# Block-sparse attention and a mixer MLP on one core: steps of two key chunks, and QK in 64-row tiles with the mask as a product

## The chip, the cores and the metric

The kernel runs on one core of a Trainium2 chip. The time is device microseconds of one execution on that core, from three timed runs; beside them stands one profiled execution, from which all durations of instructions come. TensorE (PE in the profile; PEld is its weight load) multiplies matrices into PSUM, ScalarE (ACT) and VectorE (DVE) work elementwise and are the two that empty PSUM, GpSimd (POOL) issues the casting loads, and SyncE (SP) issues the other transfers, among them the transposes by the DMA crossbar.

## The reference

Inputs q, k, v have shape (4, 8, 768, 64): 4 batches, 8 heads, 768 positions, 64 dimensions. Positions form 24 blocks of 32.

```python
scores = scale * np.matmul(q, k.transpose(0, 1, 3, 2))        # scale = 1/8
mask = np.abs(blk_i - blk_j) <= 1
mask = mask | (blk_i == 0) | (blk_j == 0) | (blk_i == 23) | (blk_j == 23)
for qb in range(24):
    for kb in sampled_blocks[qb]:                             # 3 random blocks
        mask[qb*32:(qb+1)*32, kb*32:(kb+1)*32] = True
attn = softmax(np.where(mask, scores, -1e9))
x = (attn @ v), heads side by side                            # (4, 768, 512)
h = np.maximum(x.transpose(0, 2, 1) @ w_tok1, 0) @ w_tok2     # token MLP, 768 -> 256 -> 768
u = x + h.transpose(0, 2, 1)
out = u + np.maximum(u @ w_ch1, 0) @ w_ch2                    # channel MLP, 512 -> 1536 -> 512
```

## The kernel before

**Attention** goes by pairs of heads, 16 pairs (`p`), four to a batch. q and k of a pair are loaded as bf16, brought into layout on VectorE (L533, `klay`, `qlay`), turned by TensorE (L593) and copied out of PSUM by VectorE, each head by itself, into rows 0 to 63 of `ktb` and `qtb` (L608). Rows 64 to 87 of both hold the mask as 24 more rows of the contraction: `ktb` has the indicator of the key's block, `qtb` has -30000 where the query may not see the block and 0 where it may. So one matmul over 88 rows gives masked scores. From pair 10 (`NPE`) on the turning is done by the DMA crossbar instead (L559), out of `wide` tiles in which the mask rows were laid once (`wide_stream`, L487 to L499).

A step is `(p, half, j)`: one key chunk of 128 (`j`, six of them) against 384 queries, for both heads. QK (L639) puts the transposed scores, keys in rows, into `ps`, two matmuls of 384 columns; ScalarE takes the exponential into `et` (L648, 768 elements a row, no maximum subtracted). PV (L692) then takes `et` as weights, 128 queries at a time, against v with a column of ones (65 columns), and accumulates in `po` over the six key chunks: six matmuls a step. After the sixth, VectorE takes the reciprocal of the sums (L706) and multiplies it in (L707), which gives `x`.

**The MLP** of a batch: the token MLP by halves of the channels (`tok`, L770, L795, addition L803), turning of `u` (for the first batch by TensorE, L824, later by crossbar, L750), then the channel MLP (`ch`): 96 matmuls of 384 columns (L862) with ReLU on ScalarE (L734) or VectorE (L736), and 72 of 512 columns (L888) with the residual addition on VectorE (L897) and the output transfer.

**The order of the instructions** is found when the program is built. A planner (`Planner`) plays the engines with assumed costs in ns and emits an instruction when its inputs and its buffer would be ready. TensorE takes the ready stream of lowest number: QK 0, PV 1, transposes 2, token MLP 3, channel MLP 4. The other engines take the ready operation with the lowest `prio`; ScalarE takes nothing but exponentials while one is pending (`exp_pending`). On the chip the order of each engine stays as it was planned, and semaphores hold an instruction whose inputs are late.

**Buffers:** `ps` two tiles of two PSUM banks, `po` one, `pm` three banks for everything else on TensorE; `et` eight tiles (`NET`); `ktb`, `qtb`, `vaug` four pairs each (`NV`).

Of the kernel before, what the change touches and what calls it, by code (L numbers as in the profile page):

```python
# [169 lines left out]
def kernel(  # L170
# [22 lines left out]
    NET = 8  # L193
    NPE = 10
    NL = 2
# [16 lines left out]
    wide = {  # L212
        (nm, n): sb1.tile([128, 2, NC, 128], BF16, name=f"{nm}wide{n}")
        for n in range(NL) for nm in ("k", "q")
    }

# [211 lines left out]
    wide_there = {(nm, n): Ev() for nm in ("k", "q") for n in range(NL)}  # L428
# [49 lines left out]
    def wide_stream():  # L478

        box, done, rel = {}, Ev(), Ev()  # L480

        def emit():
            P.take("pm", rel)
            box["m"] = psM.tile([128, 2, NC, 24], FP32, tag="pm", name="pm_wide")
            for i, rhs in enumerate((ident[R, 64:88], t2add[R, :])):
                for c in range(NC):
                    nc.tensor.matmul(  # L487
                        out=box["m"][:, i, c, :], lhsT=ind[R, c, :], rhs=rhs,
                        start=(i == 0 and c == 0), stop=(i == 1 and c == NC - 1),
                    )  # L490

        yield 500.0, [Ev(62 * US)], [("pm", 1)], emit, done
        for n in range(NL):
            for i, nm in enumerate(("k", "q")):
                def clear(eng, nm=nm, n=n):
                    nc.vector.memset(wide[nm, n][:, :, :, 64:128], 0.0)

                def copy(eng, nm=nm, n=n, i=i):
                    nc.vector.tensor_copy(  # L499
                        out=wide[nm, n][:, :, :, 64:88],  # L500
                        in_=free(box["m"][:, i, 0, :], 0, [[0, 2], [24, NC], [1, 24]]),
                    )
                ev = P.op(("dve",), {"dve": 420.0}, [Ev(60 * US)], clear, prio=6)
                ev = P.op(("dve",), {"dve": 450.0}, [done, ev], copy, prio=6)
                wide_there[nm, n].same_as = ev
                rel.same_as = ev

# [12 lines left out]
    def relayout(p):  # L520
        lays = {}
        for nm in ("k", "q", "v") if p else ("v",):
            raw = raws.pop((nm, p))
            arr = arrive.pop((nm, p))

            def emit(eng, nm=nm, raw=raw):
                if nm == "v":
                    nc.vector.tensor_copy(out=vaug[p % NV][:, :, :, 0:64], in_=raw[:, :, :, :])  # L528
                elif p >= NPE:
                    nc.vector.tensor_copy(out=wide[nm, p % NL][:, :, :, 0:64], in_=raw[:, :, :, :])  # L530
                else:
                    lay = sbw.tile([128, NC, 2, D], BF16, tag=f"{nm}lay", bufs=1, name=f"{nm}lay{p}")
# [10 lines left out]
            if nm != "v" and p >= NPE:  # L543
                deps.append(wide_there[nm, p % NL])
                if p - NL >= NPE:
                    deps.append(xb_done[nm, p - NL])
# [5 lines left out]
    xb_done = {}  # L552

    def crossbar(p):

        lays = relayout(p)
        for nm, bufs, there in (("k", ktb, kT_there), ("q", qtb, qT_there)):
            def emit(eng, nm=nm, bufs=bufs):
                nc.sync.dma_start_transpose(  # L559
                    out=bufs[p % NV][:, :, :].rearrange("e h (c s) -> e (h c) s", c=NC),  # L560
                    in_=wide[nm, p % NL][:, :, :, :].rearrange("p h c e -> p (h c e)"),
                )
            deps = [lays[nm + "ev"]]
            if p >= NV:
                deps.append(qk_done[p - NV])
            ev = P.op(("sp",), {"sp": 1600.0}, deps, emit, prio=1, lat=5000.0)
            xb_done[nm, p] = ev
            there[p, 0], there[p, 1] = ev, ev

    def transposes(p):  # L570
# [15 lines left out]
        for nm, bufs, there in (("k", ktb, kT_there), ("q", qtb, qT_there)):  # L586
            box, last, rel = {}, Ev(), Ev()
            for c in range(NC):
# [10 lines left out]
                if p >= NV:  # L599
                    deps.append(qk_done[p - NV])  # L600
                yield 56.0, deps, [("pm", 1)] if c == 0 else [], emit, last if c == NC - 1 else None
            for hd in range(2):
# [15 lines left out]
    steps = [(p, half, j) for p in range(NP) for half in range(2) for j in range(NC)]  # L618
# [4 lines left out]
    for s in steps:  # L623
        et_there[s] = Ev()

    def qk_stream():
        for s in steps:
            p, half, j = s
            yield lambda p=p: (p, 1) in qT_there
            done, rel = Ev(), Ev()  # L630

            def emit(s=s, done=done, rel=rel):
                p, half, j = s
                P.take("ps", rel)
                P.take("et", et_rel[s])
                ps = psS.tile([128, 2, 512], FP32, tag="ps", name=f"ps{p}_{half}_{j}")
                for hd in range(2):
                    n = p % NV
                    nc.tensor.matmul(  # L639
                        out=ps[:, hd, 0:384], lhsT=ktb[n][0:88, hd, 128 * j : 128 * j + 128],  # L640
                        rhs=qtb[n][0:88, hd, 384 * half : 384 * half + 384],
                        start=True, stop=True,
                    )
                P.exp_pending += 1

                def exp(eng):
                    et = sbw.tile([128, 2, 384], BF16, tag="et", bufs=NET, name=f"et{p}_{half}_{j}")
                    nc.scalar.activation(  # L648
                        out=et[:, :, :], in_=ps[:, :, 0:384], func=AF.Exp, scale=0.125
                    )  # L650
                    ets[s] = et
                    P.exp_pending -= 1

                ev = P.op(("act",), {"act": 735.0}, [done], exp, prio=0, lat=80.0)
                alias(et_there[s], ev)
                alias(rel, ev)

            if p == 0:
                deps = [f_there["k", j // 3], f_there["q", half]] + [rows_there[0]] * half
            else:  # L660
                deps = [e for hd in range(2) for e in (kT_there[p, hd], qT_there[p, hd])]
                if p < NPE:
                    deps.append(rows_there[p % NV])
            yield (
                326.0, deps,
                [("ps", 1), ("et", 1)], emit, done,
            )
            if half == 1 and j == NC - 1:
                alias(qk_done[p], done)

    et_rel = {s: Ev() for s in steps}

    def pv_stream():
        for s in steps:
            p, half, j = s
            done = et_rel[s]

            def emit(s=s, done=done):
                p, half, j = s
                b, pb = p // 4, p % 4  # L680
                et = ets.pop(s)
                if j == 0:
                    rel = Ev()
                    P.take("po", rel)
                    po_of[p, half] = (
                        psO.tile([128, 2, 3, 65], FP32, tag="po", name=f"po{p}_{half}"), rel
                    )
                po, rel = po_of[p, half]
                va = vaug[p % NV]
                for hd in range(2):  # L690
                    for c in range(3):
                        nc.tensor.matmul(  # L692
                            out=po[:, hd, c, :],
                            lhsT=et[:, hd, 128 * c : 128 * c + 128],
                            rhs=va[:, hd, j, 0:65],
                            start=(j == 0 and hd == 0 and c == 0),
                            stop=(j == NC - 1 and hd == 1 and c == 2),
                        )
                if j < NC - 1:
                    return  # L700

                def norm(eng):
                    if b not in xs:
                        xs[b] = sbw.tile([128, 2, NC, 256], BF16, tag="x", bufs=B, name=f"x{b}")
                    recip = sbw.tile([128, 2, 3], FP32, tag="recip", name=f"recip{p}_{half}")
# [3 lines left out]
                            xs[b][:, pb // 2, 3 * half, 128 * (pb % 2) : 128 * (pb % 2) + 128], 0,  # L709
                            [[64, 2], [256, 3], [1, 64]],  # L710
                        ),
                        in0=po[:, :, :, 0:64],
                        in1=free(recip[:, :, :], 0, [[3, 2], [1, 3], [0, 64]]),
# [3 lines left out]
                ev = P.op(("dve",), {"dve": 760.0}, [done], norm, prio=1)  # L717
                alias(rel, ev)
                alias(x_there.setdefault((p, half), Ev()), ev)

            yield lambda p=p: p in va_there
            yield 176.0, [et_there[s], va_there[p], ones_there[p % NV]], [("po", 1)] if j == 0 else [], emit, done
            if half == 1 and j == NC - 1:
# [36 lines left out]
    def tok(b, g):  # L760
        deps = [x_there[2 * g + 4 * b + i, h] for i in range(2) for h in range(2)] + [tok1_there]
# [155 lines left out]
    for p in range(NP):  # L917
        for h in range(2):
            x_there[p, h] = Ev()
# [19 lines left out]
    P.stream(-1, wide_stream())  # L939
# [57 lines left out]
```

## Time and profile before

| | before |
|---|---|
| timed runs | 273.66, 272.22, 271.15 us; median 272.22 |
| profiled execution | 271.31 us, of which the span from first to last instruction is 269.6 |
| granted TensorE clock | 0.999 |
| busy: PE, ACT, DVE, POOL | 262.9, 184.8, 118.8, 42.2 us |
| QK (L639) | 384 matmuls of 384 columns |
| exponentials (L648) | 192 of 768 elements, 810 ns |
| PV (L692) | 1152 matmuls of 65 columns |
| channel MLP (L862, L888) | 384 of 384 columns; 276 of 512, 12 of 256, 24 of 128 |

A page of the profile gives busy time by engine, the busy share of 40 slices of the span as a digit in tenths, and the chain that ended last: the work followed back from the last instruction, at each step to what released it. A group row reads: line, engine, operation, tile written <- tiles read, shape, count | busy us of the group, mean ns of one | idle us of the engine before them, and what ended that idle time. In the chain in order of time a row is: start us, us, what. A row of windows gives for each engine its busy us and, in brackets, its instructions, in the order PE, PEld, DVE, ACT, POOL, then the granted clock, the DMA share and GB/s. Matmuls are pipelined and the end of one is modelled, so their busy times overlap, and the distance from start to start is what one costs.

### The profile page before, as it was taken

What the parts mean: (1) busy time and instruction counts of PE and PEld (TensorE: products, weight loads), DVE (VectorE), ACT (ScalarE), POOL (GpSimd) and SP (SyncE); (2) the same over time, 40 slices, a digit from 0 to 9 for tenths busy, and PEclk for the clock granted to TensorE, in tenths of its full rate; (3) what the DMA queues carried; (4) which work ended last, traced back from release to release, by engine and by line L of the source; (5) the groups of instructions that cost most, each with busy time, mean ns of one, the idle gap of its engine ahead of it and who ended that gap; (6) DMA issues with size and microseconds to landing.
All of it is one profiled execution on the core that took longest, in us unless ns stands there. A gap on an engine that the chain in (4) does not pass through costs nothing.

```text
span 269.6 us, 6198 instructions
## 1 busy us (share of the span) xinstructions
PE 262.9 (98%) x2595; PEld 170.5 (63%) x2595; DVE 118.8 (44%) x269; ACT 184.8 (69%) x274; POOL 42.2 (16%) x66
## 2 busy tenths in 40 slices
PE   8898999999999999999999999999999999999995
PEld 3476777776777767777677664565445654465444
DVE  7878878696954563634435433200231002200122
ACT  5899999999999999999999910177004750077200
POOL 8746555561221000000000000000000000000000
PEclk9999999999999999999999999999999999999999
DMA  6999999999799863971300036300122002310123
GB/s 153 187 217 202 213 201 206 202 201 137 98 202 154 164 100 74 177 80 39 62 2 2 0 61 175 116 1 2 46 109 80 0 0 86 111 41 0 41 82 113
DMA packets 48476, 27.90 MB, mean 103 GB/s; under 512 B 29696, under 2 KB 44816, under 8 KB 48448
## 3 DMA queue, kind: packets, MB, share of 16 engines
q0 software_dynamic: 15104, 12.98, 31.0%
q1 hardware_dynamic: 33072, 14.33, 22.7%
q8 instruction: 20, 0.33, 0.5%
q10 hardware_dynamic: 272, 0.20, 0.3%
q14 instruction: 8, 0.07, 0.1%
HBM read 26.74 MB, written 6.29 MB: 123 GB/s over the span
## 4 chain that ended last, share of the span: by engine, by line
PE 80%; ACT 14%; DVE 3%; issue 1%; DMA 1%; ACTq 0%; DVEq 0%
PE pm_ch L862 23%; PE pm_ch L888 22%; PE ps L639 17%; ACT et L648 14%; PE po L692 9%; PE pm_tok L795 3%; PE pm_tok L770 3%; PE ps_idle L299 2%; DMA out_dram<-o 1%; PE tk L593 1%; PE tq L593 1%; DVE ktb L608 0%; DVE qtb L402 0%; PE pm_ut L824 0%; PE pm_e L395 0%
## 5 line engine op out<-in xcount | busy, mean ns | idle before, releaser
L648 ACT ACTIVATE et<-ps 128x768 bf16<-128x768 f32 x192 | 143.7, 810 | 3.1 <-PE ps L639 1.7
L639 PE MATMUL ps<-qtb,ktb 88*128 88x384 bf16 x384 | 93.7, 325 | 1.7 <-ACT et L648 1.1
L734 ACT ACTIVATE rc<-pm_ch 128x384 bf16<-128x384 f32 x74 | 36.3, 491 | 59.3 <-PE pm_ch L862 43.3
L862 PE MATMUL pm_ch<-uT,w_ch 128*128 128x384 bf16 x384 | 72.2, 326 | 0.0
L692 PEld LDWEIGHTS <-et 128*128 128x128 bf16 x1152 | 55.3, 97 | 21.6 <-DVE x L707 1.5
L888 PE MATMUL pm_ch<-w_ch,rc 128*128 128x512 bf16 (+2 forms) x312 | 63.4, 363 | 0.0
L692 PE MATMUL po<-vaug,et 128*128 128x65 bf16 x1152 | 60.4, 193 | 0.4 <-DVE x L707 0.4
L897 DVE TENSOR_TENSOR o<-pm_ch,x 128x512 f32<-128x512 f32 x23 | 15.9, 692 | 88.4 <-PE pm_ch L888 88.4
L888 PEld LDWEIGHTS <-rc 128*128 128x128 bf16 x312 | 29.6, 98 | 31.8
L862 PEld LDWEIGHTS <-w_ch 128*128 128x128 bf16 x384 | 36.2, 98 | 20.9
L639 PEld LDWEIGHTS <-ktb 88*128 88x128 bf16 x384 | 35.0, 98 | 11.6 <-issue 3.0
L803 DVE TENSOR_TENSOR x<-pm_tok,x 128x512 bf16<-128x512 f32 x24 | 15.9, 686 | 11.3 <-PE pm_tok L795 11.2
L707 DVE TENSOR_TENSOR x<-po,recip 128x384 bf16<-128x384 f32 x32 | 17.8, 557 | 1.1
L736 DVE TENSOR_SCALAR rc<-pm_ch 128x384 bf16<-128x384 f32 x22 | 12.2, 553 | 12.5 <-PE pm_ch L862 12.4
L795 PE MATMUL pm_tok<-a_t,w_tok 128*128 128x256 bf16 x96 | 17.1, 276 | 0.0
L706 DVE RECIPROCAL recip<-po 128x6 f32<-128x6 f32 x32 | 6.3, 196 | 23.7 <-PE po L692 23.0
L770 PE MATMUL pm_tok<-x,w_tok 128*128 128x256 bf16 x96 | 16.5, 272 | 0.0
L235 POOL DMA_DIRECT2D vraw<-in_v_dram x16 | 11.6, 725 | 18.6 <-DVE vaug L528 14.5
L235 POOL DMA_DIRECT2D qraw<-in_q_dram x15 | 11.0, 730 | 9.7 <-DVE qwide L530 1.6
L235 POOL DMA_DIRECT2D kraw<-in_k_dram x15 | 10.8, 717 | 8.7 <-DVE recip L706 2.4
L608 DVE COPY ktb<-tk 64x768 bf16<-64x768 bf16 x18 | 9.9, 552 | 3.0 <-PE tk L593 2.8
L795 PEld LDWEIGHTS <-w_tok 128*128 128x128 bf16 x96 | 9.8, 129 | 1.2
(73 smaller groups left out, 103.5 us busy)
## 6 DMA issues: line engine op xcount, KB each, us to landing
out_dram<-o SPq DMA_DIRECT2D x23, 256.0 KB, 2.0
vraw<-in_v_dram POOLq DMA_DIRECT2D x16, 192.0 KB, 7.7
w_ch<-in_moe_w_ch_dram POOLq DMA_DIRECT2D x8, 384.0 KB, 9.8
kraw<-in_k_dram POOLq DMA_DIRECT2D x15, 192.0 KB, 8.6
qraw<-in_q_dram POOLq DMA_DIRECT2D x15, 192.0 KB, 8.0
w_tok<-in_moe_w_tok_dram POOLq DMA_DIRECT2D x2, 384.0 KB, 9.9
kf<-in_k_dram SPq DMA_DIRECT2D x2, 192.0 KB, 3.0
ktb<-ktb SPq DMA_DIRECT2D x3, 72.0 KB
```

Of the source, the lines that this page charges most:

```text
L235: nc.gpsimd.dma_start(out=raw[:, :, :, :], in_=APx(src, 2 * p * S * D, [[NC * D, 128], [S * D, 2], [1, NC * D]]),)
L639: nc.tensor.matmul(out=ps[:, hd, 0:384], lhsT=ktb[n][0:88, hd, 128 * j : 128 * j + 128], rhs=qtb[n][0:88, hd, 384 * half : 384 * half + 38 ...
L648: nc.scalar.activation(out=et[:, :, :], in_=ps[:, :, 0:384], func=AF.Exp, scale=0.125)
L692: nc.tensor.matmul(out=po[:, hd, c, :], lhsT=et[:, hd, 128 * c : 128 * c + 128], rhs=va[:, hd, j, 0:65], start=(j == 0 and hd == 0 and c = ...
L707: nc.vector.tensor_tensor(out=free(xs[b][:, pb // 2, 3 * half, 128 * (pb % 2) : 128 * (pb % 2) + 128], 0, [[64, 2], [256, 3], [1, 64]],), ...
L734: nc.scalar.activation(out=o(), in_=i, func=AF.Relu)
L770: nc.tensor.matmul(out=box["pm"][:, t, :], lhsT=w_tok1[:, sc, 128 * t : 128 * t + 128], rhs=xs[b][:, g, sc, :], start=(t == 0 and sc == 0) ...
L795: nc.tensor.matmul(out=ubox["pm"][:, i, :], lhsT=w_tok2[:, t, :, 2 * s2 + i], rhs=a_t[:, t, :], start=(i == 0 and t == 0), stop=(i == 1 an ...
L803: nc.vector.tensor_tensor(out=st[b]["u"][:, g, 2 * s2 : 2 * s2 + 2, :], in0=ubox["pm"][:, :, :], in1=xs[b][:, g, 2 * s2 : 2 * s2 + 2, :], ...
L862: nc.tensor.matmul(out=pbox["pm"][:, 0:384], lhsT=w_ch1[:, dmc, 128 * cc : 128 * cc + 128], rhs=st[b]["uT"][:, dmc // 2, 3 * sh : 3 * sh + ...
L888: nc.tensor.matmul(out=pbox["pm"][:, 0:n], lhsT=box["rc"][:, cc, 128 * sc : 128 * sc + 128], rhs=w_ch2[:, cc, lo : lo + n], start=(cc == 0 ...
L897: nc.vector.tensor_tensor(out=o[:, :].rearrange("p (g e) -> p g e", g=2), in0=pbox["pm"][:, :].rearrange("p (g e) -> p g e", g=2), in1=st[ ...
```

## The change

A step becomes `(p, t, jj)`: two key chunks (256 keys) against 256 queries, three by three steps a pair. An exponential covers 1024 elements, a PV step has eight matmuls, and `po` is finished three times a pair. In pairs 0 to 5 QK is as before in kind: matmuls over 88 rows, four of 256 columns.

From pair 6 (`NT0`) on the mask rows are gone. `ktb` and `qtb` hold one head in rows 0 to 63 and the other in rows 64 to 127, so a transposed pair is copied out of PSUM at once, and the crossbar of pairs 10 to 15 turns the plain layout. A QK matmul covers 64 rows; the two heads' matmuls lie in different row halves of the array and write different PSUM banks. Two steps are issued together, when both `ps` tiles are free. After the exponential VectorE multiplies `et` in place by a mask of 0 and 1 (the cut, rank 5, the lowest). The mask (128 keys x 6 chunks x 768 queries) is built once, from 34 us of the planner's time on, by 12 matmuls over the 24 mask rows and 12 comparisons on VectorE; everything that overwrites the mask rows waits for it. The wide tiles go. `et` has seven tiles (of 1024 elements) for eight (of 768), and the layout tiles two buffers each for one.

```diff
-    NET = 8
+    NET = 7
     NPE = 10
-    NL = 2
+    NT0 = 6
...
+    def mask_stream():
+        for j in range(NC):
+            for hf in range(2):
...
+                    nc.tensor.matmul(
+                        out=box["m"][:, 0:384], lhsT=ind[R, j, :],
+                        rhs=qtb[0][R, 0, 384 * hf : 384 * hf + 384], start=True, stop=True,
                     )
+                yield 162.5, [Ev(34 * US), rows_there[0]], [("pm", 1)], emit, last
...
+                    nc.vector.tensor_scalar(
+                        out=mask[:, j, 384 * hf : 384 * hf + 384], in0=box["m"][:, 0:384],
+                        scalar1=-1.0, scalar2=None, op0=ALU.is_ge,
+                    )
+                ev = P.op(("dve",), {"dve": 556.0}, [last], copy, prio=4)
...
-            if nm != "v" and 2 <= p < NPE:
-                deps.append(qT_there[p - 1, 1])
+            if nm != "v" and p >= 3:
+                deps.append(qT_there[p - 2, 1])
...
                 nc.sync.dma_start_transpose(
-                    out=bufs[p % NV][:, :, :].rearrange("e h (c s) -> e (h c) s", c=NC),
-                    in_=wide[nm, p % NL][:, :, :, :].rearrange("p h c e -> p (h c e)"),
+                    out=bufs[p % NV][:, 0, :].rearrange("e (c s) -> e c s", c=NC),
+                    in_=lays[nm][:, :, :, :].rearrange("p c h d -> p (c h d)"),
                 )
-            ev = P.op(("sp",), {"sp": 1600.0}, deps, emit, prio=1, lat=5000.0)
+            deps = [lays[nm + "ev"], mask_there, qk_done[p - NV]]
+            ev = P.op(("sp",), {"sp": 900.0}, deps, emit, prio=1, lat=5000.0)
...
+            if p >= NT0:
+                def evac(eng, buf=bufs[p % NV], box=box):
+                    copy = nc.scalar.copy if eng == "act" else nc.vector.tensor_copy
+                    copy(out=buf[:, 0, :], in_=box["t"][:, :, :].rearrange("p c s -> p (c s)"))
...
-    steps = [(p, half, j) for p in range(NP) for half in range(2) for j in range(NC)]
+    steps = [(p, t, jj) for p in range(NP) for t in range(3) for jj in range(3)]
...
+    def scores(s, done, rel):
...
+        for i in range(2):
+            for hd in range(2):
+                rows, h = (slice(0, 88), hd) if p < NT0 else (slice(64 * hd, 64 * hd + 64), 0)
+                nc.tensor.matmul(
+                    out=ps[:, hd, 256 * i : 256 * i + 256],
+                    lhsT=ktb[n][rows, h, 256 * jj + 128 * i : 256 * jj + 128 * i + 128],
+                    rhs=qtb[n][rows, h, 256 * t : 256 * t + 256],
+                    start=(i == 0), stop=(i == 1),
+                )
...
+            nc.scalar.activation(out=et[:, :, :], in_=ps[:, :, :], func=AF.Exp, scale=0.125)
...
+        ev = P.op(("act",), {"act": 948.0}, [done], exp, prio=0, lat=80.0)
+        if p >= NT0:
+            def cut(eng):
+                nc.vector.tensor_tensor(
+                    out=ets[s][:, :, :].rearrange("k h (i q) -> k h i q", i=2),
+                    in0=ets[s][:, :, :].rearrange("k h (i q) -> k h i q", i=2),
+                    in1=free(mask[:, 2 * jj, 256 * t : 256 * t + 256], 0, [[0, 2], [S, 2], [1, 256]]),
+                    op=ALU.mult,
+                )
+            ev = P.op(("dve",), {"dve": 740.0}, [ev, mask_there], cut, prio=5)
...
+                yield (
+                    436.0, qk_deps(*s), [("ps", 1), ("et", 1)],
...
+            def emit(s=s, s2=s2, evs=evs):
+                scores(s, evs[0][0], evs[1][0])
+                scores(s2, evs[0][1], evs[1][1])
...
+            yield 650.0, qk_deps(*s) + qk_deps(*s2), [("ps", 2), ("et", 2)], emit, None
...
-    P.stream(-1, wide_stream())
+    P.stream(1.8, mask_stream())
```

More of the change, by code (lines that the diff above doesn't have):

```diff
@@ L476, in first_rest, with emit, copy @@
             )
[L478 to L486, printed above, removed]
+    mask = sb1.tile([128, NC, S], BF16, name="mask")
+    mask_there = Ev()
+    def mask_stream():
+        for j in range(NC):
+            for hf in range(2):
+                box, last, rel = {}, Ev(), Ev()
+                def emit(j=j, hf=hf, box=box, rel=rel):
+                    P.take("pm", rel)
+                    box["m"] = psM.tile([128, 512], FP32, tag="pm", name=f"pm_mask_{j}_{hf}")
                     nc.tensor.matmul(
-                        out=box["m"][:, i, c, :], lhsT=ind[R, c, :], rhs=rhs,
-                        start=(i == 0 and c == 0), stop=(i == 1 and c == NC - 1),
-                    )
[L492 to L501, printed above, removed]
-                    )
-                ev = P.op(("dve",), {"dve": 420.0}, [Ev(60 * US)], clear, prio=6)
-                ev = P.op(("dve",), {"dve": 450.0}, [done, ev], copy, prio=6)
-                wide_there[nm, n].same_as = ev
+                        out=box["m"][:, 0:384], lhsT=ind[R, j, :],
+                        rhs=qtb[0][R, 0, 384 * hf : 384 * hf + 384], start=True, stop=True,
+                    )
+                yield 162.5, [Ev(34 * US), rows_there[0]], [("pm", 1)], emit, last
+                def copy(eng, j=j, hf=hf, box=box):
+                    nc.vector.tensor_scalar(
+                        out=mask[:, j, 384 * hf : 384 * hf + 384], in0=box["m"][:, 0:384],
+                        scalar1=-1.0, scalar2=None, op0=ALU.is_ge,
+                    )
+                ev = P.op(("dve",), {"dve": 556.0}, [last], copy, prio=4)
                 rel.same_as = ev
+        mask_there.same_as = ev
     def act_cost(n):
@@ L624, with exp @@
         et_there[s] = Ev()
+    et_rel = {s: Ev() for s in steps}
+    def scores(s, done, rel):
+        p, t, jj = s
+        P.take("ps", rel)
+        P.take("et", et_rel[s])
+        ps = psS.tile([128, 2, 512], FP32, tag="ps", name=f"ps{p}_{t}_{jj}")
+        n = p % NV
+        for i in range(2):
+            for hd in range(2):
+                rows, h = (slice(0, 88), hd) if p < NT0 else (slice(64 * hd, 64 * hd + 64), 0)
[5 more added lines that the diff above has]
+                )
+        P.exp_pending += 1
+        def exp(eng):
+            et = sbw.tile([128, 2, 512], BF16, tag="et", bufs=NET, name=f"et{p}_{t}_{jj}")
+            nc.scalar.activation(out=et[:, :, :], in_=ps[:, :, :], func=AF.Exp, scale=0.125)
+            ets[s] = et
+            P.exp_pending -= 1
+        ev = P.op(("act",), {"act": 948.0}, [done], exp, prio=0, lat=80.0)
+        alias(rel, ev)
+        if p >= NT0:
+            def cut(eng):
[6 more added lines that the diff above has]
+            ev = P.op(("dve",), {"dve": 740.0}, [ev, mask_there], cut, prio=5)
+        alias(et_there[s], ev)
@@ L626, in qk_stream, with qk_deps @@
+    def qk_deps(p, t, jj):
+        if p > 0:
+            deps = [e for hd in range(2) for e in (kT_there[p, hd], qT_there[p, hd])]
+            return deps + [rows_there[p % NV]] * (p < NT0)
+        deps = [f_there["k", int(jj > 0)], f_there["q", int(t > 0)]]
+        return deps + [rows_there[0]] * (t > 0)
     def qk_stream():
-        for s in steps:
-            p, half, j = s
+        todo = list(steps)
+        while todo:
+            s = todo.pop(0)
+            p, t, jj = s
             yield lambda p=p: (p, 1) in qT_there
[L630 to L669, printed above, removed]
@@ L671 @@
-    et_rel = {s: Ev() for s in steps}
+            if p < NT0:
+                done, rel = Ev(), Ev()
+                yield (
+                    436.0, qk_deps(*s), [("ps", 1), ("et", 1)],
+                    lambda s=s, done=done, rel=rel: scores(s, done, rel), done,
+                )
+                if (t, jj) == (2, 2):
+                    alias(qk_done[p], done)
+                continue
+            s2 = todo.pop(0)
+            yield lambda p=s2[0]: (p, 1) in qT_there
+            evs = [Ev(), Ev()], [Ev(), Ev()]
@@ L687, in emit @@
                     )
-                po, rel = po_of[p, half]
+                po, rel = po_of[p, t]
                 va = vaug[p % NV]
[L690 to L698, printed above, removed]
@@ L699, in emit @@
-                if j < NC - 1:
+                for i in range(2):
+                    for hd in range(2):
+                        for c in range(2):
+                            nc.tensor.matmul(
+                                out=po[:, hd, c, :],
+                                lhsT=et[:, hd, 256 * i + 128 * c : 256 * i + 128 * c + 128],
+                                rhs=va[:, hd, 2 * jj + i, 0:65],
+                                start=(jj == 0 and i == 0 and hd == 0 and c == 0),
+                                stop=(jj == 2 and i == 1 and hd == 1 and c == 1),
+                            )
@@ L704, in norm @@
                         xs[b] = sbw.tile([128, 2, NC, 256], BF16, tag="x", bufs=B, name=f"x{b}")
-                    recip = sbw.tile([128, 2, 3], FP32, tag="recip", name=f"recip{p}_{half}")
+                    recip = sbw.tile([128, 2, 2], FP32, tag="recip", name=f"recip{p}_{t}")
                     nc.vector.reciprocal(out=recip[:, :, :], in_=po[:, :, :, 64])
@@ L760, in tok @@
     def tok(b, g):
[L761 removed]
+        deps = [x_there[2 * g + 4 * b + i, h] for i in range(2) for h in range(3)] + [tok1_there]
         box = {}
@@ L917 @@
     for p in range(NP):
-        for h in range(2):
-            x_there[p, h] = Ev()
+        for t in range(3):
+            x_there[p, t] = Ev()
     def tr_stream():
```

54 lines of the change are left out of this document (25 added, 29 removed).

## The prediction

> **What bounds the kernel now.** I began with the page: the busy shares, the slices and the chain that ended last.
>
> ```profile
> span 269.6 us, 6198 instructions
> PE 262.9 (98%) x2595; PEld 170.5 (63%) x2595; DVE 118.8 (44%) x269; ACT 184.8 (69%) x274; POOL 42.2 (16%) x66
> ...
> DVE  7878878696954563634435433200231002200122
> ACT  5899999999999999999999910177004750077200
> ...
> PE 80%; ACT 14%; DVE 3%; issue 1%; DMA 1%; ACTq 0%; DVEq 0%
> ```
>
> The reader is to see two stages. ScalarE is full for 22 or 23 of 40 slices (to about 153 us), which is attention; after that it is not. The chain is 80% TensorE. But a busy matmul row overlaps its neighbours, so 98% alone does not prove that TensorE is the bound. The chain in order of time does, because there every piece is the time from one start to the next:
>
> ```profile
> 42.91 0.82 ACT et L648
> ...
> 99.95 0.33 PE ps L639 x2
> ...
> 101.79 0.18 PE po L692 x6
> ...
> 102.81 0.22 PE pm_tok L770 x2
> ...
> 172.96 15.60 PE pm_ch L862 x96
> 188.56 15.54 PE pm_ch L888 x72
> ```
>
> To 43 us the chain runs through the exponentials, which are spaced by ScalarE; in the stretch from 80 to 153 us, and in everything behind it, it runs through matmuls back to back. A step of QK (two matmuls of 384 columns) takes 0.33 us, six PV matmuls 0.18 us, two of 256 columns 0.22 us, and the channel MLP of one batch 15.60 + 15.54 = 31.1 us. From 153 us on nothing but matmuls is on the path. So a microsecond of matmul time taken out of attention shortens the kernel, as long as the planner has MLP matmuls to fill the freed place. The profiled execution took 271.31 us, 1.7 us beside its span of 269.6; the median of the three timed runs is 272.22, 0.9 above it. I sum against 271.3 and add that difference, rounded to 0.6, at the end.
>
> **QK, the saving.** In pairs 0 to 5 a step has 4 matmuls of 256 columns: 54 steps x 0.44 (twice the 0.22 above) = 23.8 us, for 72 x 0.33 = 23.8 now: nothing. In pairs 6 to 15 there are 120 steps now, 120 x 0.33 = 39.6 us. Afterwards there are 45 blocks of 8 matmuls. If the two heads, in rows 0-63 and 64-127, run beside each other, the 8 cost 4 x 0.11 = 0.44 us. Entering and leaving the 64-row arrangement costs something, and only one place of this trace changes the rows of the array in mid-stream, the mask rows of the wide tiles (24 rows):
>
> ```profile
> 62.51 1.12 DVE L608 COPY ktb<-tk 64x768 bf16<-64x768 bf16 x2 [1.80 <-PE tk L593]
> ...
> 63.14 0.48 PE L639 MATMUL ps<-qtb,ktb 88*128 88x384 bf16 x2
> 63.69 0.31 PE L487 MATMUL pm_wide<-ident,ktb 24*128 24x24 bf16 x6
> 63.85 0.29 PE L487 MATMUL pm_wide<-t2add,ktb 24*128 24x24 bf16 x6
> 64.08 0.50 PE L639 MATMUL ps<-qtb,ktb 88*128 88x384 bf16 x2
> ```
>
> The QK step at 63.14 has issued its columns by 63.47 (0.33), the small matmuls start at 63.69: 0.22 us for the entry, an upper end, because their buffer was released by VectorE only at 63.63 (62.51 + 1.12). They follow each other by 0.16 / 6 = 0.027 us, are through by 64.01, and QK goes on at 64.08: 0.07 us for the exit. So a pair of changes costs 0.14 (entry like exit) to 0.29 us. I take 0.22, the middle, since the wait for the buffer explains part of the entry but not surely all. A block is 0.66 us, 45 x 0.66 = 29.7, **-9.9 us**. The ends are 45 x 0.58 = 26.1 (-13.5) and 45 x 0.73 = 32.9 (-6.7); no row shows two matmuls side by side, and if they don't, the end is 45 x (0.88 + 0.29) = 52.7, +13.1.
>
> The Trainium skill speaks against the change here ("TensorEngine Tiling (Array Packing)", Key Properties): a change of the tiling mode, not of the tile, drains TensorE. It gives no price there; from the 128 cycles of array depth in "TensorE: Matmul & The Clock Gate", Part 2, two drains are an estimated 0.11 us a block, by which the sum would be -15 instead of -9.9. The rows at 63 us show the drain's sign, but a higher upper end.
>
> **Mask and wide tiles.** The mask adds 12 matmuls of 384 columns over 24 rows: 12 x (0.16 + 0.22) = 4.6 us, from 3.6 to 5.4 by the ends above. The wide tiles' 0.61 us (63.47 to 64.08) goes. The mask stream starts at 34 us, where ScalarE still ends the chain and TensorE has a little room; I let 1 us lie there: **+3 us**. The mask ranks ahead of the transposes and the token MLP and takes PSUM buffers that VectorE frees at a low rank, so these two queue behind it. PV: 1152 matmuls before and after, nothing.
>
> **ScalarE.**
>
> ```profile
> L648 ACT ACTIVATE et<-ps 128x768 bf16<-128x768 f32 x192 | 143.7, 810 | 3.1 <-PE ps L639 1.7
> L734 ACT ACTIVATE rc<-pm_ch 128x384 bf16<-128x384 f32 x74 | 36.3, 491 | 59.3 <-PE pm_ch L862 43.3
> ```
>
> 810 - 491 ns for 384 elements more is 0.83 ns each; at 1024 elements an exponential lasts 810 + 213 = 1023 ns. They are spaced by 143.7 / 192 = 748 ns, so 961 then. In the ScalarE-bound first four pairs 48 x 0.748 = 35.9 becomes 36 x 0.961 = 34.6: **-1 us**. From pair 6 on a block of QK waits for both score buffers. The first of its exponentials can't start before half a block is done, so ScalarE stands idle for 0.33 us and two hand-overs in every block, an estimated 0.6 in 2.5: 45 x 2.5 = 113 us instead of 120 x 0.748 = 90. That alone moves the end of attention from 153 to about 175 us. It costs nothing while TensorE has MLP work, and a ReLU of L734 (0.49) fits into each gap. Behind a late block on TensorE stand PV and MLP matmuls, since its order is fixed at build time.
>
> **VectorE, the new load.**
>
> ```profile
> L707 DVE TENSOR_TENSOR x<-po,recip 128x384 bf16<-128x384 f32 x32 | 17.8, 557 | 1.1
> L897 DVE TENSOR_TENSOR o<-pm_ch,x 128x512 f32<-128x512 f32 x23 | 15.9, 692 | 88.4 <-PE pm_ch L888 88.4
> L736 DVE TENSOR_SCALAR rc<-pm_ch 128x384 bf16<-128x384 f32 x22 | 12.2, 553 | 12.5 <-PE pm_ch L862 12.4
> L608 DVE COPY ktb<-tk 64x768 bf16<-64x768 bf16 x18 | 9.9, 552 | 3.0 <-PE tk L593 2.8
> L706 DVE RECIPROCAL recip<-po 128x6 f32<-128x6 f32 x32 | 6.3, 196 | 23.7 <-PE po L692 23.0
> L528 DVE COPY vaug<-vraw 128x768 bf16<-128x768 bf16 x16 | 5.6, 351 | 0.6 <-DMA vraw<-in_v_dram 0.6
> L496 DVE MEMSET kwide<- 128x384 uint32 x2 | 0.8, 378 | 0.1
> L499 DVE CAST qwide<-pm_wide 128x288 bf16<-128x288 f32 x2 | 0.9, 442 | 0.0
> L469 DVE COPY qtb<-qtb 24x1536 bf16<-24x1536 bf16 x1 | 0.6, 552 | 0.0
> L904 DVE TENSOR_TENSOR o<-pm_ch,x 128x256 f32<-128x256 f32 x1 | 0.4, 425 | 0.6 <-PE pm_ch L888 0.6
> ```
>
> The cut is a two-operand product of 1024 elements, all 16-bit and in SBUF, and no row has one. Copies of that kind cost 0.26 ns an element (552 - 351 over 768) beside 150 ns: 420 ns is the low end. Products with a 32-bit operand in PSUM cost 1.05 ns an element (692 - 557 over 128) beside 153: 1230 ns is the high end. I take twice the copy's rate, because it is the copy's kind with twice the reading: 0.53 x 1024 + 150 = **690 ns**, and 90 x 0.69 = 62 us of VectorE. The Trainium skill ("VectorE: DVE Perf Modes", The perf-mode tier table) gives 1224 ns for 2048 such elements, an estimated 0.69 us here; no run so far shows it.
>
> The rest of VectorE: normalisation 48 x (0.196 + 0.425) = 29.8 for 32 x 0.753 = 24.1, +5.7; mask copies 12 x 0.553 = +6.6; in pairs 6 to 9 two copies of 128 rows replace four of 64, 8 x 0.55 = -4.4; wide tiles' clears and casts 4 x 0.38 + 4 x 0.44 = -3.3. In all 118.8 + 62 + 4.6 = 185 us. The copies into layout stay 351 ns, and the crossbar transposes of pairs 10 to 15 halve in size; SP and POOL stand waiting in between, and loads run four pairs ahead: nothing.
>
> Does this hold up TensorE? Attention need only be over when all other matmuls are used up. Behind it stand the token MLP of the last two pairs (about 6 us with its VectorE work) and the last batch's channel MLP (31.1), the transposes and the output (7): 44 us. For an end at 265 us that means by 221 us.
>
> ```profile
> 40.00:50.00 10.00, 9.92 (x145) 7.82 (x143) 8.84 (x21) 9.97 (x15) 4.45 (x7) 1.00 1.26 205
> ...
> 60.00:80.00 20.00, 19.78 (x285) 14.85 (x282) 14.75 (x36) 19.47 (x28) 4.53 (x7) 1.00 0.98 148
> 80.00:153.00 73.00, 72.89 (x947) 53.99 (x945) 35.81 (x80) 72.43 (x98) 0.72 (x1) 1.00 0.48 81
> ```
>
> The third busy number of these windows is VectorE's. From 60 to 153 us it does 14.8 + 35.8 = 50.6 us; with the changes above (-4, from the last ten pairs) and the output additions of three batches that now fall into attention (18 x 0.69 = 12.4) it is 59, and 121 with the cuts. At 88% full, the most that a window shows (8.84 of 10), that takes 138 us: attention ends at about 198 us, 23 us early enough. The cut is hidden up to (161 x 0.88 - 59) / 90 = 0.92 us each. But the fixed orders now have to mesh with three full engines: for PV matmuls that wait for a late cut, with QK blocks queued behind them, I add **+2 us** (0 to 6).
>
> **Sum:** 271.3 - 9.9 + 3 - 1 + 2 = 265.4, with the 0.6 of the median **266**.
>
> **Rivals.** *The cut goes at one element a cycle, 1.23 us.* For it: every two-operand row of this trace goes so. Against: none of those is 16-bit in SBUF. It decides from 0.92 us: 90 x 1.23 + 59 = 170 us of VectorE after 60 us, attention ends between 230 (always full) and 253 us (88%), no MLP is left to fill, and 44 us follow: 274 to 297, about 281. **Slower.** *The heads do not run side by side:* block 0.88 + 0.22 = 1.10, 45 x 1.10 - 39.6 = +9.9, 271.3 + 9.9 + 3 - 1 + 2 + 0.6 = 286; nothing here excludes it. *Given back:* the saving is there, but a full VectorE releases PSUM buffers and exponentials late, TensorE idles by 5 to 9 us in attention instead of 2, mask switches at the upper end: 269 to 275, about 271. For it: VectorE goes from 50% to 88% in that stage; against: between 80 and 153 us, with ScalarE as full as that, the chain has hardly a wait.
>
> **How the numbers follow.** Forecast 0.55, given back 0.25, slow cut 0.12, no overlap 0.08. The likeliest case alone runs from 260 (-13.5 and no stall) to 269. The range for 8 in 10 goes on through "given back" into the slow cut, to 279, and leaves out the no-overlap case, most of the slow cut and a little at the low end. Within 1% (269.5 to 275), about what a measurement of this kernel can tell from no change, lies most of "given back" (0.21) and a sliver of the forecast (0.02); slower are the two slow cases and the rest of "given back", 0.23; faster 0.54.
>
> **What the profile after would show.** QK blocks 0.58 to 0.73 us from start to start of what follows, with the second head's matmul starting within tens of ns of the first's; above 1 us the overlap is wrong. Cuts of 0.69 us x90; 1.23 makes the first rival right. Mask matmuls of 4 to 5 us with their changes. ScalarE no longer full from pair 6 on, with ReLUs between the exponentials. Attention ending at 175 to 200 us, and MLP matmuls back to back behind it for 60 to 80 us instead of 109; if they are back to back for less than 45, VectorE has become the bound. What would make me wrong: changes of the array's rows dearer than 0.29, the tok or transposes starved by the mask between 34 and 55 us, or waits of PV for cuts beyond 6 us.

## The result, and the profile after

The changed kernel takes 265.39 us (264.44 to 265.68), the kernel before beside it 272.0: a ratio of 0.9744, 95% interval 0.9691 to 0.9797. In a second job it took 264.8 us, ratio 0.9753 (0.9736 to 0.977). The forecast was 266. The profiled execution took 265.54 us with a span of 263.8. One execution of the first experiment below (278.72 us, of four) ran in a slower state of the chip and is left out of its time and ratio.

The page of the changed kernel, the lines that answer to those of before:

```profile
span 263.8 us, 6585 instructions
PE 254.3 (96%) x2769; PEld 167.2 (63%) x2787; DVE 173.1 (66%) x387; ACT 178.4 (68%) x226; POOL 42.1 (16%) x66
...
DVE  7978968697989789788879798888850013200221
ACT  5789999998887887677777887777317720277000
...
PE 87%; DVE 4%; ACT 3%; DMA 2%; issue 1%; SPq 0%; DVEq 0%; ACTq 0%
```

ScalarE is no longer full from the tenth slice on, VectorE is at 6 to 9 tenths, mostly 8, to the 29th (190 us), and the chain lies on TensorE for 87% instead of 80. Its pieces in order of time, one QK block and then the end:

```profile
101.08 0.24 PE po L719 x8
101.32 0.16 PE pm_ch L889
101.48 0.54 PE ps L633 x8
102.02 0.43 PE pm_ch L889 x2
...
192.74 1.31 PE pm_tok L797 x12
...
196.73 15.85 PE pm_ch L889 x96
212.85 10.74 PE pm_ch L915 x49
...
228.12 15.60 PE pm_ch L889 x96
...
257.43 3.39 DMA out_dram<-o
```

Eight matmuls of 256 columns lie between two starts 0.54 us apart, where eight of 0.11 would need 0.88. In the records the matmuls of the two heads start 0.003 us apart and the pairs 0.109 us. So 0.436 of the 0.54 are columns and the rest is the exit. The entry stands in front of the block, as the starts in the timeline show (the first number of a row):

```profile
101.15 0.33 PE L889 MATMUL pm_ch<-uT,w_ch 128*128 128x384 bf16 x1
101.41 0.61 PE L633 MATMUL ps<-qtb,ktb 64*128 64x256 bf16 x8
101.96 0.50 PE L889 MATMUL pm_ch<-uT,w_ch 128*128 128x384 bf16 x2
```

From the MLP matmul to the block it is 0.26 us, where such a matmul otherwise takes 0.163: 0.096 for the entry. (The chain counts this 0.1 us to the row behind the block, 0.43 for two matmuls.)

From the token MLP of the last heads (192.7 us) on, MLP matmuls run for 64 us, to 256.7; before, by the same rows, it was 108 (155.4 to 263.8). (A few of the matmul records of L915 are missing, so x49 is not the full count.) The last output took 3.39 us to land, 2.05 before: 1.3 us of the end that no step of the change explains. It took 3.63 us in the second profile of this kernel, and 2.04 in that of the kernel without cuts below.

The groups by form, and the longest wait of ScalarE:

```profile
L643 ACT ACTIVATE et<-ps 128x1024 bf16<-128x1024 f32 x144 | 138.9, 1023 | 29.9 <-PE ps L633 28.9 <-DVE x L734 0.4
L651 DVE TENSOR_TENSOR et<-et,mask 128x1024 bf16<-128x1024 bf16 x90 | 57.8, 682 | 0.0
L734 DVE TENSOR_TENSOR x<-po,recip 128x256 bf16<-128x256 f32 x48 | 20.4, 424 | 1.7
L733 DVE RECIPROCAL recip<-po 128x4 f32<-128x4 f32 x48 | 8.7, 181 | 20.4 <-PE po L719 20.1
L484 PE MATMUL pm_mask<-qtb,ktb 24*128 24x384 bf16 x12 | 3.5, 329 | 0.0
```

```profile
ACT et L643 <- PE ps L633: 28.9, 47, 1.4
```

### The profile page after: what moved, and what is told of

It reads as the page before. It is cut to its first block, busy times and chain, and to the rows that moved or that the text cites. A ratio compares the mean times of both kernels' runs of the same rounds, so it can differ in the third digit from the quotient of the medians.

```text
span 263.8 us, 6585 instructions
## 1 busy us (share of the span) xinstructions
PE 254.3 (96%) x2769; PEld 167.2 (63%) x2787; DVE 173.1 (66%) x387; ACT 178.4 (68%) x226; POOL 42.1 (16%) x66
## 4 chain that ended last, share of the span: by engine, by line
PE 87%; DVE 4%; ACT 3%; DMA 2%; issue 1%; SPq 0%; DVEq 0%; ACTq 0%
PE pm_ch L889 24%; PE pm_ch L915 22%; PE ps L633 17%; PE po L719 13%; PE pm_tok L797 4%; PE pm_tok L822 4%; ACT et L643 3%; DMA out_dram<-o 1%; PE tk L575 1%; DMA kf<-in_k_dram 1%; PE pm_mask L484 1%; DVE x L830 1%; DVE et L651 1%; PE tq L575 1%; DVE o L924 0%
## 5 line engine op out<-in xcount | busy, mean ns | idle before, releaser
L643 ACT ACTIVATE et<-ps 128x1024 bf16<-128x1024 f32 x144 | 138.9, 1023 | 29.9 <-PE ps L633 28.9
L915 PE MATMUL pm_ch<-w_ch,rc 128*128 128x512 bf16 (+2 forms) x294 | 67.0, 362 | 1.1 <-issue 0.3
L633 PE MATMUL ps<-qtb,ktb 64*128 64x256 bf16 (+1 forms) x576 | 61.2, 274 | 1.4 <-ACT et L643 1.2
L719 PEld LDWEIGHTS <-et 128*128 128x128 bf16 x1152 | 49.9, 98 | 16.3 <-issue 3.0
L651 DVE TENSOR_TENSOR et<-et,mask 128x1024 bf16<-128x1024 bf16 x90 | 57.8, 682 | 0.0
L719 PE MATMUL po<-vaug,et 128*128 128x65 bf16 x1152 | 56.3, 194 | 0.6 <-DVE et L651 0.2
L633 PEld LDWEIGHTS <-ktb 64*128 64x128 bf16 (+1 forms) x576 | 33.0, 96 | 19.4 <-issue 13.9
L915 PEld LDWEIGHTS <-rc 128*128 128x128 bf16 x312 | 27.5, 97 | 24.8 <-issue 1.3
L733 DVE RECIPROCAL recip<-po 128x4 f32<-128x4 f32 x48 | 8.7, 181 | 20.4 <-PE po L719 20.1
L734 DVE TENSOR_TENSOR x<-po,recip 128x256 bf16<-128x256 f32 x48 | 20.4, 424 | 1.7
L797 PE MATMUL pm_tok<-x,w_tok 128*128 128x256 bf16 x96 | 13.4, 273 | 0.0
L230 POOL DMA_DIRECT2D kraw<-in_k_dram x15 | 10.8, 718 | 7.8 <-DMA w_tok<-in_moe_w_tok_dram 2.7
L230 POOL DMA_DIRECT2D qraw<-in_q_dram x15 | 10.8, 723 | 6.6 <-DVE klay L524 1.2
```

Source lines behind the costliest of these rows:

```text
L230: nc.gpsimd.dma_start(out=raw[:, :, :, :], in_=APx(src, 2 * p * S * D, [[NC * D, 128], [S * D, 2], [1, NC * D]]),)
L633: nc.tensor.matmul(out=ps[:, hd, 256 * i : 256 * i + 256], lhsT=ktb[n][rows, h, 256 * jj + 128 * i : 256 * jj + 128 * i + 128], rhs=qtb[n] ...
L643: nc.scalar.activation(out=et[:, :, :], in_=ps[:, :, :], func=AF.Exp, scale=0.125)
L651: nc.vector.tensor_tensor(out=ets[s][:, :, :].rearrange("k h (i q) -> k h i q", i=2), in0=ets[s][:, :, :].rearrange("k h (i q) -> k h i q" ...
L719: nc.tensor.matmul(out=po[:, hd, c, :], lhsT=et[:, hd, 256 * i + 128 * c : 256 * i + 128 * c + 128], rhs=va[:, hd, 2 * jj + i, 0:65], star ...
L734: nc.vector.tensor_tensor(out=free(xs[b][:, pb // 2, 2 * t, 128 * (pb % 2) : 128 * (pb % 2) + 128], 0, [[64, 2], [256, 2], [1, 64]],), in0 ...
```

## The experiments

Each ran beside the kernel before on its chip. Differences from the changed kernel are taken by ratio: 0.9753 times the before of the same job.

**Only the new step shape** (no 64-row tiles, no cut, one step at a time).

```diff
--- before
-    steps = [(p, half, j) for p in range(NP) for half in range(2) for j in range(NC)]
+    steps = [(p, t, jj) for p in range(NP) for t in range(3) for jj in range(3)]
```

(Scores, PV and normalisation are as in the change, with `NT0 = 16`, so all pairs go over 88 rows.)

> The kernel before with one part of the change alone: steps of two key chunks by 256 queries, everywhere with the mask rows (88 rows) and one step at a time, the wide tiles kept. My theory (the gain is TensorE time of QK from pair 6 on): QK stays 144 x 0.44 = 63 us of columns as before, ScalarE's exponentials go from 192 x 0.748 = 144 us to 144 x 0.96 = 138 us, which only the first four pairs show, 1.3 us; VectorE gains 5.7 us of normalisation where it has room. So 270 to 272 us, within 1% of before. Rival (the gain is ScalarE's, from fewer and longer exponentials): 5.3 us less, 266 to 267, nearly all of the change.

276.12 us, ratio 1.0161 (1.0122 to 1.02): theory and rival both missed. ScalarE's 5 us of shorter work bring nothing, so the rival falls. But the step alone is also slower than before, by 4.4 us by ratio, which my theory did not have. Part of it is one halt. The chain of this kernel:

```profile
73.63 8.70 DMA kraw<-in_k_dram
82.33 0.35 DVE qwide L531
82.68 0.60 DVE a_t L767
```

A copy of q (L531) stood in VectorE's fixed order ahead of a ReLU of the token MLP and waited, and TensorE with it, from 80.8 to 83.3 us: 2.5 of the 4.4 us. The chain names a load of k, but the semaphores of the copy say otherwise. Its own load was issued at 56.7 us; what came last, at 82.2, was the landing of a crossbar transpose issued at 70.8, which reads the same wide tile that the copy overwrites. The rest was not traced. So the gain comes from the other half of the change.

**No overlap**: both heads' matmuls in rows 0 to 63.

```diff
--- after
-                rows, h = (slice(0, 88), hd) if p < NT0 else (slice(64 * hd, 64 * hd + 64), 0)
+                rows, h = (slice(0, 88), hd) if p < NT0 else (slice(0, 64), 0)
...
-            yield 650.0, qk_deps(*s) + qk_deps(*s2), [("ps", 2), ("et", 2)], emit, None
+            yield 1080.0, qk_deps(*s) + qk_deps(*s2), [("ps", 2), ("et", 2)], emit, None
```

> The changed kernel in which from pair 6 on the matmuls of both heads use rows 0 to 63 (the first head's data twice; the second head's scores are left out), so that no two can run beside each other. All other instructions are as in the changed kernel, and the planner is told 1.08 us for a block. Theory (the two halves run beside each other, and that is the gain): a block grows by 4 x 0.108 = 0.43 us, 45 x 0.43 = +19.5 us, 283 to 287 us, slower than the kernel before. Rival (the halves never overlapped, and the gain lies elsewhere): 264 to 267 us.

283.3 us, 1.0435 (1.0415 to 1.0454), 18.5 us more than the changed kernel. The chain shows the block itself, 0.98 for 0.54:

```profile
101.13 0.98 PE ps L633 x8
```

0.44 x 45 = 19.8 us. Without the overlap the change would be 4% slower than before. This is the prediction's second slow rival, priced there at 286.

**One head after the other**, the same matmuls in another order.

```diff
--- after
-                scores(s, evs[0][0], evs[1][0])
-                scores(s2, evs[0][1], evs[1][1])
+                for part in range(2):
+                    scores(s, evs[0][0], evs[1][0], part)
+                    scores(s2, evs[0][1], evs[1][1], part)
```

(Each call issues the matmuls of head `part` alone.)

> The changed kernel with the matmuls of a block in another order: first head's four, then the second head's four, so that matmuls that follow one another lie in the same half of the rows and only one neighbour pair can overlap. Theory (the overlap of the two halves is the gain): a block lasts 7 x 0.108 + 0.1 instead of 4 x 0.108 + 0.1, 45 x 0.32 = +14.6 us, and some more by later exponentials: 279 to 283 us. Rival (the trace's near-equal starts are modelled, the halves do not truly overlap): no change, 265 us.

266.12 us, 0.9815 (0.979 to 0.9841): 1.6 us more, not 15. My expectation failed, and the rival's reason is refuted by the run above. The chain shows a block as before:

```profile
100.97 0.55 PE ps L636 x8
```

In program order six of the seven distances between starts would have to be 0.108, and the block 0.86. Here the starts of one block go by 0.013, 0.107, 0.013, 0.096 us, and the waits and signals on them tell which is which: the second head's matmuls, four places later in the program, run 0.013 us behind the first head's.

**One step at a time**, 90 blocks of four.

```diff
--- after
+            done, rel = Ev(), Ev()
+            yield (
+                432.0, qk_deps(*s), [("ps", 1), ("et", 1)],
+                lambda s=s, done=done, rel=rel: scores(s, done, rel), done,
+            )
...
+            continue
```

> The changed kernel with one step of QK at a time from pair 6 on, so 90 blocks of 4 matmuls instead of 45 of 8, and 45 more entries and exits of the 64-row arrangement. In the trace after, an entry costs 0.096 us and an exit about 0.10, so my theory is 45 x 0.2 = +9 us, 273 to 275. The rival is that TensorE has spare time and what counts is ScalarE's idle gap in every block of two steps (28.9 us in all in the trace after), which goes here: then 260 to 265.

272.94 us, 1.0062 (1.0044 to 1.008): 8.5 us more, near the theory's 9. A block of four takes 0.32 to 0.33 us from start to start:

```profile
100.11 0.32 PE ps L633 x4
...
101.11 0.33 PE ps L633 x4
...
103.67 0.54 PE ps L633 x8
```

That is 0.218 of columns and 0.10 for the exit, and 0.096 more stands in front of it. The last row shows what the expectation left out: two blocks can stand directly behind each other and share their changes. Seven pairs of blocks do in the profiled execution, so there are 83 visits, 38 more than 45, and 38 x 0.19 = 7.2 us; the other 1.3 us were not traced. ScalarE's idle time, shorter here, gave nothing back.

**The cut done twice**, and **a quarter more of it**.

```diff
--- after
+                nc.vector.tensor_tensor(
+                    out=ets[s][:, :, :].rearrange("k h (i q) -> k h i q", i=2),
+                    in0=ets[s][:, :, :].rearrange("k h (i q) -> k h i q", i=2),
+                    in1=free(mask[:, 2 * jj, 256 * t : 256 * t + 256], 0, [[0, 2], [S, 2], [1, 256]]),
+                    op=ALU.mult,
+                )
```

(The lines shown stand behind the same product in the changed kernel. In the second kernel the added product covers columns 0 to 127 of each head's 512. The planner is told 1480 and 1050 ns.)

> The changed kernel with every cut done twice (the second product by 0 and 1 changes nothing), 1.36 us of VectorE a step instead of 0.68. By the prediction's working VectorE has 59 + 90 x 1.36 = 182 us to do after 60 us, so attention ends between 242 (always full) and 267 us (88% full) and 44 us follow: 286 to 311 us. If VectorE is off the path even then, 265; if only half of the added 61 us is exposed, about 290.

> The changed kernel in which a quarter of each cut is done a second time (256 of 1024 elements, some 0.28 us), 0.96 us of VectorE a step instead of 0.68. The prediction has the cut hidden up to 0.92 us: 0.96 puts the end of attention at 60 + (59 + 86) / 0.88 = 225 us for 221, so 1 to 5 us more than the changed kernel, 266 to 270. If VectorE binds from much less on, 275 to 283, on the line from 265 (0.68) to 302 (1.36).

Twice: 301.75 us, 1.1112 (1.1074 to 1.115). A quarter more: 269.0 us, 0.9915 (0.9888 to 0.9943), 4.3 us more than the changed kernel. Both are within what was expected. The chain of the second one shows what the edge looks like:

```profile
222.47 1.31 PE pm_tok L802 x12
...
227.35 3.67 DMA uT<-x
231.07 15.44 PE pm_ch L894 x94
246.50 12.96 PE pm_ch L920 x60
```

The last token MLP begins at 222.5 us, and its crossbar transpose lies open on the path: no MLP of the third batch is left to cover it. Until there the excess is hidden, and behind it most of it counts: from the second kernel to the first VectorE has 36 us more of cuts (62.3 added for 26.3), and the time grows by 32.5 us, some of it through a lower clock (last section). VectorE's fill, the third busy number:

```profile
80.00:140.00 60.00, 60.00 (x649) 36.08 (x646) 53.00 (x124) 41.90 (x58) 2.87 (x4) 1.00 0.41 83
140.00:200.00 60.00, 60.00 (x664) 36.35 (x663) 53.58 (x123) 41.33 (x52) 0.00 (x0) 1.00 0.17 45
```

88 and 89%, the fill that the prediction took for full.

**No cut.**

```diff
--- after
-        if p >= NT0:
+        if False:
```

> The changed kernel without the 90 cuts (the mask is left out in pairs 6 to 15; it is still built). 58 us of VectorE go, and PV follows the exponential directly. Theory (the cuts are hidden behind other matmuls; the prediction let 2 us of TensorE waits stand for them): 0 to 2 us less, 263 to 266 us. Rival (a VectorE full at 85% in attention gives back part of the gain): 4 to 8 us less, 257 to 261 us.

263.76 us, 0.9727 (0.9682 to 0.9773), against 0.9753: 0.7 us less, which this run cannot tell from nothing. The 58 us of cuts are covered.

**The mask out of masked scores**, in two jobs.

```diff
--- after
-                        out=box["m"][:, 0:384], lhsT=ind[R, j, :],
-                        rhs=qtb[0][R, 0, 384 * hf : 384 * hf + 384], start=True, stop=True,
+                        out=box["m"][:, 0:384], lhsT=ktb[0][0:88, 0, 128 * j : 128 * j + 128],
+                        rhs=qtb[0][0:88, 0, 384 * hf : 384 * hf + 384], start=True, stop=True,
...
-                        scalar1=-1.0, scalar2=None, op0=ALU.is_ge,
+                        scalar1=-15000.0, scalar2=None, op0=ALU.is_ge,
```

> The changed kernel with the mask built from masked scores: the 12 matmuls cover rows 0 to 87 of the first buffer (head 0's k and q and the mask rows) and VectorE compares with -15000 instead of -1, so TensorE keeps its 128-row arrangement. What goes is the change of the arrangement around the mask matmuls, in nine places in the trace after, some 0.2 to 0.25 us each: 1.8 to 2.3 us at most, less what lies in ScalarE-bound time. Theory: 1 to 2 us less, 263 to 264.5. Rival (mask matmuls lie in free time altogether): 265 to 266.

> The kernel with the mask built from masked scores once more, now beside the changed kernel on the same chip. Theory (nine pairs of changes of 0.2 us gone, and nothing else): 1.2 to 2.2 us less than the changed kernel. If the 2.4 us between the two earlier jobs was the chip's and not the edit's: less than 1 us.

262.94 us (0.9685, 0.9667 to 0.9702), then 263.74 us (0.9718, 0.9697 to 0.9739) beside the changed kernel's 264.8:

> The changed kernel itself, on the same chip and beside the same runs of before as the three that follow: 264.5 to 266 us, to measure them against.

So 1.9 us less by ratio in the first job, and about 1 us, 0.4%, in the pair on one chip. That is under the 1.2 to 2.2 of the second expectation, and the intervals of the two overlap a little. It is the fastest version of the study, and the chain of the changed kernel shows what it takes away:

```profile
36.09 0.42 PE pm_mask L484 x2
...
41.43 0.26 PE pm_mask L484
```

A mask matmul alone takes 0.26 us to the next start, 0.16 of it columns and 0.10 the exit; the entry stands in front of it as with a block.

**Tiles from pair 4**, and **from pair 8**.

```diff
--- after
-    NT0 = 6
+    NT0 = 4
...
-                yield 162.5, [Ev(34 * US), rows_there[0]], [("pm", 1)], emit, last
+                yield 162.5, [Ev(22 * US), rows_there[0]], [("pm", 1)], emit, last
```

(The other kernel changes `NT0` alone, to 8.)

> The changed kernel with the 64-row tiles from pair 4 on instead of 6, the mask begun at 22 us of the planner's time instead of 34. TensorE saves 2 x (9 x 0.44 - 4.5 x 0.64) = 2.2 us more; VectorE has 18 cuts = 12.3 us more, in a stretch (43 to 60 us) in which it is 80% busy already. Theory (TensorE time alone counts as long as there is MLP work): 263 to 264 us. Rival (there is none yet in that stretch, since the first batch's token MLP has only just ended, and VectorE is late): 266 to 270.

> The changed kernel with the 64-row tiles from pair 8 on instead of 6. TensorE loses 2 x (9 x 0.44 - 4.5 x 0.64) = 2.2 us, VectorE has 18 cuts = 12.3 us less. Theory (what TensorE saves is what counts): 2 us more than the changed kernel, 266.5 to 268.5. Rival (VectorE's fill costs as much as the tiles save): no change or less, 263 to 265.5.

From 4: 265.63 us, 0.9776 (0.9751 to 0.9801), no gain where 2 us were expected; the rival's 266 to 270 was not reached either. In this kernel the stretch from 43 to 60 us reads:

```profile
43.00:60.00 17.00, 15.27 (x238) 11.97 (x236) 15.10 (x36) 14.60 (x16) 8.08 (x12) 1.00 1.29 203
```

In the changed kernel it reads:

```profile
43.00:60.00 17.00, 17.00 (x264) 14.67 (x263) 13.53 (x34) 16.44 (x18) 8.43 (x13) 1.00 1.29 203
```

With the tiles from 4 VectorE is 89% full for 80%, and TensorE, without a pause in the changed kernel, has 1.7 us without a matmul: the first batch's MLP isn't ready, and the cover that later stages have is missing. (What the earlier mask alone does in this kernel was not separated.) From 8: 265.63 us, 0.9795 (0.9775 to 0.9814), 1.1 us more than the changed kernel: the sign of the theory and about half of its 2 us.

## Why the prediction was right, step by step

- **The bound.** Right: TensorE's time decides as long as MLP matmuls are left to fill, shown by the blocks of four and of one half, which add TensorE time (+8.5 and +18.5 us for 7.2 and 19.8 of it), and more weakly by the kernels that take some away or give some back (mask over 88 rows, tiles from pair 8: about half of the time counted). With tiles from pair 4 it did not hold: there was no MLP to fill.
- **QK block**, 0.66 us predicted: 0.54 + 0.096 = 0.64. The entry, bounded by 0.22, is 0.096; so by this the rest of that bound was the wait for the buffer. The exit is 0.093 (0.07 taken from the small matmuls). Saved are 39.6 - 45 x 0.64 = 10.8 us for 9.9. The estimate of two drains from the Trainium skill ("TensorEngine Tiling (Array Packing)", Key Properties, with the 128 cycles of "TensorE: Matmul & The Clock Gate", Part 2) was 0.11 a block, and 0.19 is measured.
- **Mask**, +3: mis-sized in its parts. Its 12 matmuls and nine pairs of changes (some stand in twos) cost 12 x 0.16 + 9 x 0.2 = 3.7 us for 4.6, less 0.6 for the wide tiles 3.1, and I had let 1 us of it be covered; the 88-row mask recovered 1.1 of 1.8 by the medians, so part was.
- **ScalarE.** 1023 ns predicted, 1023 measured. The idle time in the blocks was set at 0.6 x 45 = 27 us, and 28.9 are there, off the path.
- **VectorE.** The cut: 690 ns predicted, 682 measured; the Trainium skill's rate for two 16-bit operands ("VectorE: DVE Perf Modes", The perf-mode tier table) agrees, also with the mask read once for each head. In the records cuts that follow one another start 0.60 us apart, so a cut costs VectorE less than its 0.68; its whole busy time was summed to 185 us and is 173. Reciprocal and product: 621 ns predicted, 605 measured.
- **End of attention**, 198 us predicted: the last token MLP starts at 192.7, since VectorE had 113 us to do from 60 us on, not 121. The edge was put at 0.92 us a cut; at 0.97 (0.68 and 0.29) the transpose lay open and 4.3 us were lost. No run lies between 0.68 and 0.97, so the edge itself is not measured. At 1.37 the answer lay within 286 to 311, a range that had no lower clock in it.
- **Waits**, +2, and -1 in the first four pairs: the span fell by 5.8 us; 10.8 saved and 3.1 spent would be 7.7, so 1.9 us were lost, 1.3 of them in the last transfer. A lower granted clock from 8 to 43 us (0.95; 1.00 in the second profile, whose span is 263.1) may be part of the rest. The +2 stood for PV matmuls that wait for cuts, and without the cuts 0.7 us went, which cannot be told from nothing. So this term was probably too large, and the last transfer, which no term had, took its place: that the sum came within 1 us is in part luck. The -1 was not measured by itself.

## What to carry to other kernels

When a matmul-bound stretch has a contraction of 64 rows, two of them in the two halves of the array cost one, and the price is the change of arrangement, 0.2 us a visit here: make each visit long, and count it against the columns saved. Work moved to an engine with room is free only while something else fills the bound engine, so work out the edge (here the moment when the last batch's MLP stands alone) and not the mean fill. A part that shortens an engine off the path, like the longer exponentials here, may be worth nothing by itself.

## What the runs showed of the hardware

The two row halves take their matmuls independently of program order: in the kernel with one head after the other, a half ran matmuls that stood four places behind those of the other half, 0.013 us after them, and eight took 0.55 us where program order allows no less than 0.86. And where TensorE was left waiting, the granted clock fell: with the cut done twice its mean was 0.932, and in these stretches, in which TensorE was busy for 87% of the time, it was 0.93 and 0.83 (the number behind POOL's). With a quarter more of the cut, where TensorE stayed full from 80 to 200 us, it was 1.00. With the tiles from pair 4, where TensorE stood without a matmul for 1.7 of 17 us, it was 1.00 too. So the fall goes with long waiting here, and what sets it was not tested.

```profile
140.00:190.00 50.00, 43.50 (x448) 25.59 (x446) 45.24 (x82) 28.35 (x35) 0.00 (x0) 0.93 0.22 57
190.00:210.00 20.00, 17.41 (x177) 10.59 (x178) 17.88 (x33) 13.07 (x19) 0.00 (x0) 0.83 0.11 20
```
